# A Fourier mixer with two channel mixtures on one core: loads reordered behind the head, the second batch's first stage one spectral step sooner, decodes at other steps, all first-mixture statistics held

## The chip, the cores and the metric

The kernel runs on one core of a Trainium2 chip. The metric is device time in microseconds (us), the median of repeated executions. The profile shows one execution of the kernel before.

## What is computed

`x` has the shape (2, 3136, 256), in float32. Three blocks follow each other:

```python
X = rfft(x, axis=1)                                  # attention-like spectral filter
Y = soft(X.real@w_r - X.imag@w_i + b_r) + 1j*soft(X.real@w_i + X.imag@w_r + b_i)   # soft: shrink by 0.01
x = irfft(Y, n=3136, axis=1)
xn = (x - mean) / sqrt(var + 1e-6) * g_ln            # first mixture ("first MLP")
x = x + relu(xn @ w_ch1) @ w_ch2
u = x + real(fft(fft(x, axis=1), axis=2))            # second mixture
out = u + relu(norm(u) @ w2_ch1) @ w2_ch2
```

The mixture weights arrive as float64 words, and the kernel takes them apart into a high and a low float32 part itself ("decode").

## The kernel before, in words

The length 3136 is factored as 49 times 64. The work runs in this order on TensorE (PE), which is the engine that is nearly always busy.

1. **Head, stage 1 of batch 0.** `Forward` loads eight tiles of `x` (98 x 1024) and multiplies each half with the table `cam` (L331, plain float32, two passes each); VectorE (DVE) transposes the result out of PSUM (L333). Two steps of batch 1 (`fw[1]`, tiles named `q`) follow in the same plain form.
2. **Spectral steps.** The loop over `NS` = 26 steps calls `p2_step(i)`: `p2_b` multiplies two frequencies of the first stage with the table `cb` (L499, into one of three `psa` buffers) and splits the result into a high part (ScalarE, ACT) and a low part (DVE, L218); `p2_mix` of the step two before multiplies with the split filter weights `wm` (24 matmuls L532, into one of two `psb` buffers), and DVE adds the bias (L538) and clips (L539), GpSimd (POOL) subtracts (L218, `h<-w`); `p2_inv` of the step three before multiplies with `ci` (L553, into one of three `psc` buffers). A `psb` buffer is free again when its L538 is done.
3. **What rides along in that loop.** The dictionary `todo` hangs work on steps: `CONST_AT` the loads of tables (`cb`, `ci`, biases) and of `fw[1]` tiles, `MLP1_AT` the eight decodes of the first mixture's weights (`load_mlp`: a load `s64` of 512 KB, L569, then eight DVE instructions L581 to L589, function `decode64`). `behind` puts them after the latest clip and POOL subtraction that the program has marked. `STAGE1_AT[i]` says how many steps of stage 1 of batch 1 come in step i: each is split into `c` high (ACT) and `c` low (POOL) and multiplied in three matmuls (L228, L229, L230). The `q` tiles have three buffers, the `c` tiles four.
4. **First mixture.** 13 chunks of 3 or 4 tiles of 128 rows (`mlp1`), handled by `run_mlp`: `l1` is 8 groups of 6 matmuls (L228 to L230, into `psa`), each evacuated by ACT (L765) and then DVE (L767); `l2` is L784 and L785. While chunk k runs, the statistics (L664, L665), the normalisation (L672 to L676, applied by L691/L692 on ACT or L696 on DVE) and the flip (L705) of chunk k+2 are made. They hang on named places of chunk k; the table `EARLY` (chunks 11 and 12) places the statistics at the first two groups, `PLAIN` and `SHORT` (the others) later.
5. Stage 4 (98-row transforms, L228 to L230 into `psc`, L467 to L472) rides along from chunk 8, and the second mixture follows.

What puts instructions in order: a scheduler in the framework places each instruction on its engine by a modelled time, within the bounds of data, buffers and `tc.issue_after(...)`. Each engine then works strictly in that order, and so does SP, which issues all loads and stores. In `run_mlp`, `stats` is held behind the L767 of its own place by `issue_after(ch.rest[...])`, except where the plan has the key `"land"`, which only `EARLY` has.

Of the kernel before, what the change touches and what calls it, by code (L numbers as in the profile page):

```python
# [17 lines left out]


ZERO_AT = 12  # L20
STAGE1_AT = (0, 0, 0, 0, 2, 2, 2, 2, 2, 2, 2, 0)
STAGE3_FROM = 16
STAGE3_AT = (0,) * 16 + (4, 4, 4, 4)
CONST_AT = (0, 0, 1, 2, 2, 3, 4, 5, 6, 8)
MLP1_AT = (3, 8, 11, 12, 14, 15, 22, 23)
MLP2_AT = ((3, 7), (4, 2), (4, 7), (5, 2), (5, 7), (6, 4), (11, 1), (12, 3))
STAGE3_MLP = tuple((0, "l1", i) for i in (4, 5, 6, 7)) + tuple((0, "l2", i) for i in range(4)) + tuple(
    (1, "l1", i) for i in (1, 3, 5, 7)) + tuple((1, "l2", i) for i in range(4))
# [142 lines left out]
def fourier_moe_kernel(ctx, tc, x, w_r, w_i, b_r, b_i, g_ln, w11, w12, w21, w22,  # L171
# [14 lines left out]
    def hslot(dt=F32R):  # L186
        return wk.tile([128, 1024], dt, tag="h", name="h", bufs=HB)

    def qslot(dt=F32R):
        return wk.tile([128, 1024], dt, tag="q", name="q", bufs=3)  # L190
# [374 lines left out]
    def load64(src3, tag):  # L565

        s64 = wk.tile([128, 512], I64, tag=tag, name="s64", bufs=2)
        o = s64 if len(src3.shape) == 2 else s64.rearrange("p (f c) -> p f c", f=src3.shape[1])
        sp.dma_start(out=o, in_=src3)  # L569
        return s64  # L570
# [20 lines left out]
    def load_mlp(w1, w2, r, tag, two):  # L591

        srcs, raw = [], {}
        for i in range(4):
            c, h = divmod(i, 2)
            srcs.append((w1[c * 128:(c + 1) * 128, h * 512:(h + 1) * 512], i * 512))
        for i in range(4):
            srcs.append((w2[i * 256:(i + 1) * 256, :].rearrange("(f p) c -> p f c", p=128), 2048 + i * 512))  # L600

        def ask(k):
            if k < 8 and k not in raw:
                raw[k] = load64(srcs[k][0], tag)

        def piece(k):
            def f():
                ask(k)
                if two:
                    ask(k + 1)  # L610
                    t1, t2 = (wk.tile([128, 512], I32, tag="t98", name="t64", bufs=TB) for _ in range(2))
                elif k > 4:
                    ask(k + 1)
                    t1, t2 = (wk.tile([128, 512], I32, tag="r98", name="t64", bufs=R98) for _ in range(2))
                else:
                    ask(k + 1)
                    t = wk.tile([128, 2, 512], I32, tag="stg", name="t64", bufs=SB)
                    t1, t2 = t[:, 0, :], t[:, 1, :]
                o = srcs[k][1]
                if k < 4:  # L620
                    v = r.rearrange("p h f -> p (h f)")
                    decode64(raw[k], v[:, o:o + 512], v[:, 2048 + o:2560 + o], t1, t2)
                else:
                    v = w_views(r)[1][:, 2 * k - 8:2 * k - 6, :]
                    decode64(raw[k], v[:, :, 0:D], v[:, :, D:2 * D], t1, t2)
            return f

        return [lambda: ask(0)] + [piece(k) for k in range(8)]
# [290 lines left out]
    fw = [Forward(0, "a", lambda: hslot(F32)), Forward(1, "c", lambda: qslot(F32))]  # L919

    def l_cb(k, n):
        sp.dma_start(out=cb[:, k:k + n, :].rearrange("p k c -> p (k c)"), in_=t_cb[:, k * 128:(k + n) * 128])

    def l_ci(k, n):
        sp.dma_start(out=ci[:, k:k + n, :].rearrange("p k c -> p (k c)"), in_=t_ci[:, k * 128:(k + n) * 128])
# [36 lines left out]

    r3 = cp.tile([128, 2, 4096], F32R, tag="r3", name="r3a")
    wv1 = w_views(r3)
    mlp1_w = load_mlp(w11, w12, r3, "o", False)[1:]
    todo = {}

    def l_ca():
# [9 lines left out]
    def l_cd():  # L978
        tab["cd"] = cp.tile([128, 2, 129], F32, tag="cd", name="cd")
        sp.dma_start(out=flat(tab["cd"]), in_=t_cd)  # L980

    consts = [lambda: l_cb(7, 3), lambda: l_ci(4, 4),
              lambda: [fw[1].load(k) for k in range(1, 4)],
              lambda: l_cb(10, 7), lambda: l_ci(8, 8),
              lambda: l_cb(17, 8), lambda: l_ci(16, 8),
              lambda: (sp.dma_start(out=cb0, in_=t_cb0),
                       sp.dma_start(out=bias0[0:34], in_=b_r.unsqueeze(0).broadcast_to([34, D])),
# [4 lines left out]
              lambda: (l_cb(0, 1), l_ca())]  # L992
    for k, f in zip(CONST_AT, consts):
        todo.setdefault(k, []).append(f)
    for k, f in zip(MLP1_AT, mlp1_w):
        todo.setdefault(k, []).append(f)
    mlp1 = chunks1(0, wv1) + chunks1(1, wv1)
    mlp1[0].flipped = mlp1[1].flipped = False
# [20 lines left out]
    for i in range(NS + INV_BEHIND):  # L1019
        for f in todo.get(i, ()):  # L1020
            behind(f)
        for _ in range(STAGE1_AT[i] if i < len(STAGE1_AT) else 0):
            if fw[1].g % 2 == 0 and fw[1].g < 10:
# [9 lines left out]
        p2_step(i)  # L1033
        for e in range(STAGE1_AT[i + 1] if i + 1 < len(STAGE1_AT) else 0):
            with tc.issue_after(mark["hi"]), tc.issue_after(mark["pool"]):
# [25 lines left out]
    def run_mlp(chunks, nxt, hooks):  # L1061

        allc = chunks + nxt
        for k, ch in enumerate(chunks):
            n, m, far = (allc[k + d] if k + d < len(allc) else None for d in (1, 2, 3))
            at = {}

            def put(when, f, *a):
                part, i = when
                at.setdefault((part, min(i, ch.nt - 1) if part == "l2" else i), []).append(lambda: f(*a))  # L1070

            def split(c, ch=ch, n=n):
                with tc.issue_after(ch.relu), tc.issue_after(ch.rest[NF - 1]):
                    n.trans(c)

            def land(n, back):
                with ExitStack() as es:
                    if back is not None:
                        es.enter_context(tc.issue_after(back))
                    n.land()  # L1080

            if n is not None and n.flipped:
                if not n.landed:
                    put(LAND_AT, land, n, allc[k - 1].sent if k else None)
                for c in range(2):
                    put(("l2", 0), split, c)
            if m is not None:
                n_ = m
                if n_.front is not None:
                    pl = SOON if n_ is mlp2[0] else LATE if n_ is mlp2[6] else USUAL  # L1090
                    i = 0
                    for p, pr in enumerate(n_.front.pairs):
                        def stage_b(p, ch=ch, n_=n_):
                            with tc.issue_after(ch.pe):
                                n_.front.stage_b(p)

                        put(("l1", pl["b"][p]), stage_b, p)
                        put(("l1", pl["mix"][p]), n_.front.dmix, p, n_.y, i)
                        w = 2 if pr[0][1] else 1
                        for t in range(w):  # L1100
                            put(pl["stats"][p], n_.stats, i + t)
                        i += w
                else:
                    pl = EARLY if ch in mlp1[9:] else PLAIN if ch.nt == 4 else SHORT

                    def stats(t, ch=ch, n_=n_, when=pl["stats"], pl=pl):
                        with ExitStack() as es:
                            if "land" not in pl:
                                es.enter_context(tc.issue_after(ch.rest[when[t][1]]))
                            n_.stats(t)  # L1110

                    for t in range(4):
                        put(pl["stats"][t], stats, t)

                def norm(t, ch=ch, n_=n_, pl=pl):
                    with ExitStack() as es:
                        if n_.front is None and "land" not in pl:
                            es.enter_context(tc.issue_after(ch.relu))
                        if t == 0:
                            n_.norm()  # L1120
                        n_.apply(t)

                for t in range(4):
                    put(pl["norm"][t], norm, t)
                for h in range(2):
                    put(pl["flip"][h], n_.flip, h)
                if "land" in pl:
                    n_.landed = True
                    put(pl["land"], n_.land)
            soon = far is not None and far is not mlp1[6]  # L1130
            if soon:
                far.fetch()
            for f in range(NF):
                ch.l1(f)
                for h in at.get(("l1", f), []) + hooks.get((k, "l1", f), []):
                    h()
            for j in range(ch.nt):
                i = j if n is not None else ch.nt - 1 - j
                ch.l2(i)
                ch.store(i)  # L1140
                for h in at.get(("l2", j), []) + hooks.get((k, "l2", j), []):
                    h()
            if far is not None:
                if not soon:
                    far.fetch()
                if far.front is not None:
                    far.front.load()
# [123 lines left out]
```

## Time and profile before

| | |
|---|---|
| device time, median of 3 runs | 794.65 us (793.35 to 795.44) |
| the profiled execution | 795.71 us, of which the span of the trace is 793.7 us |
| PE busy | 780.3 us (98%), 4306 matmul records |
| DVE / ACT / POOL busy | 556.9 / 374.5 / 181.3 us |
| chain that ended last | PE 85%, DMA 6%, DVE 5% |

To read it: the engine with 98% bounds the kernel, so what can be gained without less arithmetic is PE's idle time and the time in which its clock is down. A busy PE is not PE at its peak, so idle time is found by the starts of neighbouring instructions and not by the busy sum alone. Times in the trace count from the start of the span.

### The profile page before, as it was taken

What the parts mean: (1) busy time and instruction counts of PE and PEld (TensorE: products, weight loads), DVE (VectorE), ACT (ScalarE), POOL (GpSimd) and SP (SyncE); (2) the same over time, 40 slices, a digit from 0 to 9 for tenths busy, and PEclk for the clock granted to TensorE, in tenths of its full rate; (3) what the DMA queues carried; (4) which work ended last, traced back from release to release, by engine and by line L of the source; (5) the groups of instructions that cost most, each with busy time, mean ns of one, the idle gap of its engine ahead of it and who ended that gap; (6) DMA issues with size and microseconds to landing.
All of it is one profiled execution on the core that took longest, in us unless ns stands there. A gap on an engine that the chain in (4) does not pass through costs nothing.

```text
span 793.7 us, 12135 instructions
## 1 busy us (share of the span) xinstructions
PE 780.3 (98%) x4306; PEld 664.4 (84%) x4306; DVE 556.9 (70%) x1253; ACT 374.5 (47%) x807; POOL 181.3 (23%) x198
## 2 busy tenths in 40 slices
PE   9899999999999999999999999999999999999997
PEld 3789987988888888988788898888888898888886
DVE  6499987678865889868765887555655757666643
ACT  0354356447954444457333336554643535444421
POOL 0176321254511111144430001566400000000000
PEclk9999999999999999999999999999999999999999
DMA  8822210630247233355643336554543334322211
GB/s 239 258 75 84 65 49 1 209 117 28 80 146 275 70 127 120 115 149 187 207 149 98 106 109 159 151 164 139 150 133 93 112 123 121 101 77 76 61 33 40
DMA packets 78911, 95.16 MB, mean 120 GB/s; under 512 B 17538, under 2 KB 59274, under 8 KB 78656
## 3 DMA queue, kind: packets, MB, share of 16 engines
q1 hardware_dynamic: 78772, 94.33, 39.2%
q8 instruction: 34, 0.56, 0.3%
q14 instruction: 25, 0.20, 0.1%
q10 hardware_dynamic: 80, 0.07, 0.0%
HBM read 56.89 MB, written 37.49 MB: 119 GB/s over the span
## 4 chain that ended last, share of the span: by engine, by line
PE 85%; DMA 6%; DVE 5%; SPq 1%; issue 1%; POOL 1%; ACT 1%; DVEq 0%; POOLq 0%
PE psb L784 23%; PE psb L785 12%; PE psa L228 11%; PE psa L229 11%; PE psa L230 11%; PE psb L532 4%; PE psc L852 3%; DMA q<-in_x_dram 2%; PE psc L230 2%; PE psc L368 2%; PE psc L228 2%; DMA s<-in_moe_w_ch_dram 2%; PE psc L229 2%; PE psc L877 1%; PE psa L499 1%; PE psc L553 1%
## 5 line engine op out<-in xcount | busy, mean ns | idle before, releaser
L765 ACT ACTIVATE h<-psa 128x512 fp32r<-128x512 f32 (+2 forms) x208 | 117.3, 572 | 199.9 <-PE psa L230 146.6
L767 DVE SCALAR_TENSOR_TENSOR h<-psa,h 128x512 fp32r<-128x512 f32 (+2 forms) x208 | 135.1, 654 | 61.1 <-ACT h L765 58.1
L784 PE MATMUL psb<-r3a,h 128*128 128x512 f32 x392 | 137.1, 395 | 0.0
L784 PE MATMUL psb<-r2b,h 128*128 128x512 f32 x392 | 136.8, 397 | 0.0
L785 PE MATMUL psb<-r3a,h 128*128 128x256 f32 x392 | 106.2, 281 | 0.0
L785 PE MATMUL psb<-r2b,h 128*128 128x256 f32 x392 | 105.9, 281 | 0.0
L532 PE MATMUL psb<-wm,h 128*128 128x256 f32 (+1 forms) x600 | 92.1, 298 | 0.6 <-DVE w L538 0.6
L532 PEld LDWEIGHTS psb<-wm,h 128*128 128x128 f32 (+1 forms) x600 | 79.0, 188 | 8.5 <-issue 6.4
L784 PEld LDWEIGHTS psb<-r2b,h 128*128 128x128 f32 x392 | 71.7, 188 | 15.7 <-issue 0.6
L784 PEld LDWEIGHTS psb<-r3a,h 128*128 128x128 f32 x392 | 71.9, 188 | 15.1
L228 PE MATMUL psa<-u0r,r3a 128*128 128x512 f32 (+1 forms) x208 | 80.0, 385 | 1.9 <-DVE h L767 1.9
L228 PE MATMUL psa<-u0r,r2b 128*128 128x512 f32 (+2 forms) x208 | 80.6, 387 | 0.0
L229 PE MATMUL psa<-u0r,r3a 128*128 128x512 f32 (+1 forms) x208 | 79.0, 381 | 0.0
L229 PE MATMUL psa<-u0r,r2b 128*128 128x512 f32 (+2 forms) x208 | 78.5, 378 | 0.0
L230 PE MATMUL psa<-u0r,r2b 128*128 128x512 f32 (+2 forms) x208 | 78.0, 380 | 0.0
L785 PEld LDWEIGHTS psb<-r3a,h 128*128 128x128 f32 x392 | 73.9, 189 | 4.0
L785 PEld LDWEIGHTS psb<-r2b,h 128*128 128x128 f32 x392 | 74.0, 189 | 3.3
L230 PE MATMUL psa<-u0r,r3a 128*128 128x512 f32 (+1 forms) x208 | 76.6, 380 | 0.0
L790 DVE TENSOR_TENSOR o<-psb,yb 128x256 f32<-128x256 f32 x74 | 30.2, 418 | 57.5 <-PE psb L785 56.2
L210 ACT ACTIVATE yg<-psc 98x512 f32<-98x512 f32 (+2 forms) x58 | 49.5, 872 | 30.4 <-PE psc L553 14.7
L218 POOL TENSOR_TENSOR u0r<-w,u0r 98x512 fp32r<-98x512 f32 (+2 forms) x28 | 37.4, 1349 | 95.5 <-ACT u0r L210 94.5
L218 POOL TENSOR_TENSOR h<-w 128x512 f32<-128x512 f32 (+1 forms) x26 | 34.7, 1334 | 93.0 <-DVE w L539 64.4
(141 smaller groups left out, 1369.8 us busy)
## 6 DMA issues: line engine op xcount, KB each, us to landing
dT<-q SPq DMA_DIRECT2D x19, 512.0 KB
q<-dT SPq DMA_DIRECT2D x19, 512.0 KB
s<-in_moe_w_ch_dram SPq DMA_DIRECT2D x16, 512.0 KB
dA<-o SPq DMA_DIRECT2D x32, 196.0 KB
dY<-yg SPq DMA_DIRECT2D x12, 512.0 KB
r<-dA SPq DMA_DIRECT2D x48, 128.0 KB
dX<-o SPq DMA_DIRECT2D x10, 512.0 KB
yb<-dX SPq DMA_DIRECT2D x50, 64.0 KB
```

The source lines that it names most:

```text
L210: nc.scalar.activation(out=o, in_=i, func=AF.Copy, scale=scale)
L218: ins = eng.tensor_tensor(out=o, in0=a, in1=b, op=ALU.subtract)
L228: nc.tensor.matmul(out=ps, lhsT=lh, rhs=rh, start=first, stop=False)
L229: nc.tensor.matmul(out=ps, lhsT=ll, rhs=rh, start=False, stop=False)
L230: ins = nc.tensor.matmul(out=ps, lhsT=lh, rhs=rl, start=False, stop=last)
L532: nc.tensor.matmul(out=ps[0:m, u * D:(u + 1) * D], lhsT=xv[:, o:o + m], rhs=wm_hl[wv][:, e, c, :], start=k == 0, stop=k == 11)
L765: ins = nc.scalar.activation(out=h[:, 0:n], in_=ps[:, 0:n], func=AF.Relu)
L767: ins = nc.vector.scalar_tensor_tensor(out=l[:, 0:n], in0=ps[:, 0:n], scalar=0.0, in1=h[:, 0:n], op0=ALU.max, op1=ALU.subtract)
L784: nc.tensor.matmul(out=ps, lhsT=h[:, ts_], rhs=w2[:, f, :], start=f == 0, stop=False)
L785: ins = nc.tensor.matmul(out=ps[:, 0:D], lhsT=l[:, ts_], rhs=w2[:, f, 0:D], start=False, stop=f == NF - 1)
L790: nc.vector.tensor_tensor(out=o, in0=ps[:, 0:D], in1=self.y[:, i, :], op=ALU.add)
L852: nc.tensor.matmul(out=ps, lhsT=self.raw[p][0:n, k, q * 128:(q + 1) * 128], rhs=self.cols(n, pr[k][1], im), start=True, stop=True)
```

## The change

It is made in four tables and three places of the code. The number of instructions on every engine stays as it was; their order moves.

- `STAGE1_AT`: the seven double steps of batch 1's stage 1 come in spectral steps 3 to 9 instead of 4 to 10.
- `CONST_AT` and `consts`: the first raw weight load (`mlp1_w[0]`) is asked for right behind `cb` 7 to 9; `fw[1].load(1)` comes before `ci` 4 to 7; loads 2 and 3 come one by one behind `cb` 10 to 16.
- `MLP1_AT`: the decodes hang on steps 3, 7, 10, 11, 12, 14 instead of 3, 8, 11, 12, 14, 15 (the last two as before).
- `stats` in `run_mlp`: the statistics of chunks 11 and 12 are now held as the others are.

```diff
-STAGE1_AT = (0, 0, 0, 0, 2, 2, 2, 2, 2, 2, 2, 0)
+STAGE1_AT = (0, 0, 0, 2, 2, 2, 2, 2, 2, 2, 0)
-CONST_AT = (0, 0, 1, 2, 2, 3, 4, 5, 6, 8)
-MLP1_AT = (3, 8, 11, 12, 14, 15, 22, 23)
+CONST_AT = (0, 0, 0, 0, 1, 1, 2, 3, 4, 5, 6, 7, 8)
+MLP1_AT = (3, 7, 10, 11, 12, 14, 22, 23)
-    mlp1_w = load_mlp(w11, w12, r3, "o", False)[1:]
+    mlp1_w = load_mlp(w11, w12, r3, "o", False)
-    consts = [lambda: l_cb(7, 3), lambda: l_ci(4, 4),
-              lambda: [fw[1].load(k) for k in range(1, 4)],
-              lambda: l_cb(10, 7), lambda: l_ci(8, 8),
+    consts = [lambda: l_cb(7, 3), mlp1_w[0], lambda: fw[1].load(1), lambda: l_ci(4, 4),
+              lambda: l_cb(10, 7), lambda: fw[1].load(2), lambda: fw[1].load(3), lambda: l_ci(8, 8),
-    for k, f in zip(MLP1_AT, mlp1_w):
+    for k, f in zip(MLP1_AT, mlp1_w[1:]):
-                            if "land" not in pl:
-                                es.enter_context(tc.issue_after(ch.rest[when[t][1]]))
+                            es.enter_context(tc.issue_after(ch.rest[when[t][1]]))
```

**Place 1, the loads on SP behind the head.** Before, from the load of `cb` 7 to 9 on (`s64` is a raw weight load, `q` a tile of batch 1):

```order
L922 DMA cb_77<-in_cb_dram 128x384
L925 DMA cw_82<-in_ci_dram 128x512
L309 DMA q_208<-in_x_dram 98x1024
L309 DMA q_210<-in_x_dram 98x1024
L309 DMA q_212<-in_x_dram 98x1024
L922 DMA cb_77<-in_cb_dram 128x896
L925 DMA cw_82<-in_ci_dram 128x1024
L922 DMA cb_77<-in_cb_dram 128x1024
L569 DMA s64_270<-in_moe_w_ch1_dram 128x512
```

And in the changed kernel, from the same load on:

```order
L922 DMA cb_77<-in_cb_dram 128x384
L569 DMA s64_196<-in_moe_w_ch1_dram 128x512
L309 DMA q_198<-in_x_dram 98x1024
L925 DMA cw_82<-in_ci_dram 128x512
L922 DMA cb_77<-in_cb_dram 128x896
L309 DMA q_213<-in_x_dram 98x1024
L309 DMA q_226<-in_x_dram 98x1024
L925 DMA cw_82<-in_ci_dram 128x1024
L569 DMA s64_279<-in_moe_w_ch1_dram 128x512
L309 DMA q_290<-in_x_dram 98x1024
```

The first raw weight load moved from eighth place behind `cb` 7 to 9 to first, and two of the three `q` loads went behind the next `cb` load.

**Place 2, the first decode on DVE.** Before, from the last split of the first three spectral steps on (the decode is L581 to L589 on `t64`):

```order
L218 TENSOR_TENSOR h_228<-psa_229,h_227 128x4x128
L538 TENSOR_TENSOR w_264<-psb_238,cw_82 128x512
L539 TENSOR_SCALAR w_265<-w_264 128x512
L581 TENSOR_SCALAR t64_274<-s64_270 128x512
L584 TENSOR_SCALAR t64_274<-s64_270 128x512
L583 SCALAR_TENSOR_TENSOR t64_274<-s64_270,t64_274 128x512
L538 TENSOR_TENSOR w_320<-psb_294,cw_82 128x512
L218 TENSOR_TENSOR h_284<-psa_285,h_283 128x4x128
```

And in the changed kernel:

```order
L218 TENSOR_TENSOR h_229<-psa_230,h_228 128x4x128
L581 TENSOR_SCALAR t64_281<-s64_196 128x512
L584 TENSOR_SCALAR t64_281<-s64_196 128x512
L583 SCALAR_TENSOR_TENSOR t64_281<-s64_196,t64_281 128x512
L585 SCALAR_TENSOR_TENSOR r3a_191<-t64_281 128x512
L586 TENSOR_SCALAR t64_281<-s64_196 128x512
L588 TENSOR_SCALAR t64_281<-r3a_191 128x512
L538 TENSOR_TENSOR w_265<-psb_239,cw_82 128x512
L587 SCALAR_TENSOR_TENSOR t64_281<-s64_196,t64_281 128x512
L539 TENSOR_SCALAR w_266<-w_265 128x512
```

Six of the eight decode instructions now stand ahead of the first bias addition L538; before, the decode stood between the first clip and the second L538. On PE the first split step of batch 1 (L228 on `c98_270`) now stands behind the 33rd of the first 40 L532 that follow the fourth `p2_b`; before, it stood behind all 40 and 27 further L532, eight L499 and two L553.

**Place 3, the statistics on DVE at the start of chunk 9 of the first mixture.** One piece of the difference; the first L767 above it is that of chunk 9's first group:

```order
-L790 TENSOR_TENSOR o<-psb,yb 128x256
-L705 STREAM_TRANSPOSE q<-q 128x4x4x32 x2
-L791 TENSOR_TENSOR o<-psb,o 128x256
-L471 TENSOR_TENSOR o_1758<-o_1758,psc 98x2x127
-L767 SCALAR_TENSOR_TENSOR h<-psa,h 128x512
-L472 TENSOR_TENSOR o_1758<-o_1758,psc 98x2x127
-L664 BN_STATS st<-yb 128x6 x3
+L664 BN_STATS st<-yb 128x6 x2
+L665 BN_AGGR mv<-st 128x2 x2
+L790 TENSOR_TENSOR o<-psb,yb 128x256
+L791 TENSOR_TENSOR o<-psb,o 128x256
```

The statistics of the three tiles of chunk 12 (`x3`) leave chunk 9 for chunk 10, and those of the four tiles of chunk 11 (`x2`, and a second `x2` behind the next L767) come from chunk 8 into chunk 9.

## Rows read from the trace of the kernel before

**Rows 1.** The page, busy time of the engines.

```profile
PE 780.3 (98%) x4306; PEld 664.4 (84%) x4306; DVE 556.9 (70%) x1253; ACT 374.5 (47%) x807; POOL 181.3 (23%) x198
```

**Rows 2.** Timeline of PE, head: start us, us, what, form, xcount [idle before <-releaser].

```profile
25.57 5.04 PE L532 MATMUL psb<-wm,h 128*128 128x256 f32 x40
30.45 0.61 PE L499 MATMUL psa<-cb,yg 128*128 128x128 f32 x4
32.70 1.16 PE L499 MATMUL psa<-cb,yg 128*128 128x128 f32 x8 [1.64 <-DMA cb<-in_cb_dram]
...
37.44 0.61 PE L499 MATMUL psa<-cb,yg 128*128 128x128 f32 x4
38.60 0.59 PE L532 MATMUL psb<-wm,h 128*128 128x256 f32 x3 [0.56 <-DVE w L538]
40.08 0.50 PE L228 MATMUL psc<-c,cam_hl 98*128 98x512 f32 x1 [0.89 <-ACT c L210]
...
46.05 0.84 PE L532 MATMUL psb<-wm,h 128*128 128x256 f32 x5
47.80 0.50 PE L228 MATMUL psc<-c,cam_hl 98*128 98x512 f32 x1 [0.91 <-ACT yg L210]
48.14 0.40 PE L229 MATMUL psc<-c,cam_hl 98*128 98x512 f32 x1
48.93 0.50 PE L230 MATMUL psc<-c,cam_hl 98*128 98x512 f32 x1 [0.40 <-POOL c L218]
```

**Rows 3.** Timeline of DVE in the same stretch.

```profile
25.29 0.69 DVE L218 TENSOR_TENSOR h<-psa,h 128x512 fp32r<-128x512 f32 x1 [0.48 <-ACT h L210]
...
28.73 0.69 DVE L538 TENSOR_TENSOR w<-psb,cw 128x512 f32<-128x512 f32 x1 [2.75 <-PE psb L532]
...
36.49 0.43 DVE L581 TENSOR_SCALAR t<-s 128x512 int32<-128x512 int32 x1 [6.61 <-DMA s<-in_moe_w_ch_dram]
...
37.77 0.68 DVE L538 TENSOR_TENSOR w<-psb,cw 128x512 f32<-128x512 f32 x1
```

**Rows 4.** The chain that ended last, in order of time: start us, us, what.

```profile
19.12 4.87 DMA cb<-in_cb_dram
24.01 12.46 DMA s<-in_moe_w_ch_dram
```

**Rows 5.** Timeline across the start of chunk 9's third group (PE, DVE).

```profile
381.37 1.08 DVE L664 BATCH_NORM_STATS2 st<-yb 128x6 f32<-128x256 f32 x3 [3.57 <-DMA yb<-dY]
...
383.92 0.39 PE L230 MATMUL psa<-u0r,r3a 128*128 128x512 f32 x1
...
385.47 0.68 DVE L767 SCALAR_TENSOR_TENSOR h<-psa,h 128x512 fp32r<-128x512 f32 x1
...
386.20 0.79 PE L228 MATMUL psa<-u0r,r3a 128*128 128x512 f32 x1 [1.89 <-DVE h L767]
...
389.72 0.39 PE L230 MATMUL psc<-u0r,ca_hl 98*98 98x512 f32 x1
```

**Rows 6.** Stretches: window, PE, PEld, DVE, ACT, POOL busy (x), PEclk, DMA, GB/s.

```profile
380.00:382.00 2.00, 2.00 (x10) 1.65 (x9) 0.63 (x2) 0.01 (x1) 0.00 (x0) 1.00 0.37 122
...
386.20:389.70 3.50, 3.50 (x8) 2.66 (x9) 3.43 (x9) 0.54 (x1) 0.56 (x1) 0.51 0.98 313
```

**Rows 7.** Timeline of DVE in chunk 10, from the end of an `l2` tile.

```profile
409.21 0.42 DVE L790 TENSOR_TENSOR o<-psb,yb 128x256 f32<-128x256 f32 x1 [1.14 <-PE psb L785]
...
411.71 0.69 DVE L767 SCALAR_TENSOR_TENSOR h<-psa,h 128x512 fp32r<-128x512 f32 x1 [0.17 <-ACT h L765]
...
413.07 0.69 DVE L767 SCALAR_TENSOR_TENSOR h<-psa,h 128x512 fp32r<-128x512 f32 x1 [0.34 <-ACT h L765]
```

**Rows 8.** One group of DVE by line, 54 to 110 us: xcount, busy us, mean ns, idle before.

```profile
L588 DVE TENSOR_SCALAR t<-r3a 128x512 int32<-128x512 int32 x5 | 4.3, 857 | 0.0
```

**Rows 9.** Timeline of DVE, one decode instruction alone and one stretched.

```profile
80.08 0.42 DVE L588 TENSOR_SCALAR t<-r3a 128x512 int32<-128x512 int32 x1
...
88.11 1.51 DVE L588 TENSOR_SCALAR t<-r3a 128x512 int32<-128x512 int32 x1
```

## The prediction

> **What bounds the kernel now.** I read the page first: PE is busy for 780.3 us of a span of 793.7 us, every other engine far less [rows 1]. The change neither adds nor takes away an instruction on any engine, so only PE's lost time can be won, and it has to be found first. A busy sum hides it, so I went through the starts of neighbouring PE instructions. Two places carry nearly all that can move: the head between 30 and 50 us, and one spot at 384 to 390 us.
>
> In the head PE waits five times, for a transfer, DVE, ACT and POOL [rows 2]. A pass of L532 takes 0.122 us (40 from 25.57 to 30.45), one of L499 0.11, one of 512 columns 0.23. From the end of the passes before to the next start, the waits are 30.89 to 32.70 (a `cb` load), 37.88 to 38.60 (DVE's L538), 38.97 to 40.08 (ACT), 46.66 to 47.80 (ACT), 48.37 to 48.93 (POOL): 1.81 + 0.72 + 1.11 + 1.14 + 0.56 = 5.34 us.
>
> Why those engines are late is told by DVE [rows 3]: it stands still for 6.61 us until a raw weight load (`s64`) lands at 36.5, because the first decode stands in its queue. The bias addition L538 behind it starts at 37.77, and the splits that ACT and POOL make for PE come late with it. The chain says the same: that load takes 12.46 us from its issue [rows 4].
>
> At the second place DVE again waits for a transfer, 3.57 us, with the statistics of chunk 12 at the head of its queue [rows 5]. The L767 behind them starts at 385.47, and PE, which needs that `psa` buffer, starts at 386.20 instead of 384.15: 2.05 us. Then the granted clock is 0.51 in the next 3.5 us, the lower of the two levels (1.2 GHz), after PE had stood still, while just before it was 1.00 [rows 6]. Eight passes from 386.20 to 389.72 take 3.52 us where the full clock needs about half, 1.80: 1.72 us more. Together 3.77 us.
>
> **The change part by part.** *Loads on SP.* Rates first. Between the landing of `cb` 7 to 9 (19.12 + 4.87 = 23.99) and that of the raw load (36.47) lie, by the order, 256 + 3 x 392 + 448 + 512 + 512 + 512 = 3416 KB in 12.48 us: 274 KB/us [rows 4]. In the new order 512 KB follow `cb` 7 to 9 at once: an estimate of 23.99 + 1.9 = 25.9 us for the first raw load. Bounds: 25.2 at half as much again per us, and 32.0 if it took 12.46 us from its issue at 19.5 as before. I take 25.9, as the queue in front of it is the same up to the load before. The `q` tile behind it: 904 KB, 27.3 us. `cb` 10 to 16: before, 1880 KB after 23.99 until PE went on at 32.70, that is 216 KB/us; now 1608 KB, so 31.4 (29.9 at 274 KB/us).
>
> The rule that speaks against this is in the Trainium skill, "DMA: Bandwidth & Descriptors", section "Queues, rings and completion order": one transfer is split over several engines' rings, and completion isn't first in, first out per issuing engine, so a place in SP's queue is no landing time. By it the load could land as late as its slowest ring; the trace agrees in part, since the late landing of `cb` 10 to 16 is slower than the mean rate. It is the first rival.
>
> *First decode.* DVE's last split ends at 25.98 [rows 3], so the load is there. Three of the six decode instructions took 1.28 us (36.49 to 37.77); the other three take another 1.3 if none is stretched, 2.4 if one is as L588 at times (0.42 alone, 1.51 stretched [rows 9]). That is 28.6 to 29.7, and the L538 behind them could not start before 28.73 anyway, when PE delivers [rows 3]. The decode fits into a 2.75 us gap in which DVE was idle; cost about 0, at most 1.0 us of DVE time. The second L538 then comes near 31.3, when PE has finished its 40 passes and the two of L228/L229 between them, instead of 37.77.
>
> *Stage 1 of batch 1 a step sooner.* PE comes to its first split matmul at 25.57 + 33 x 0.122 = 29.6; the `q` tile is there at 27.3 and needs one ACT copy, room 1.6 us. PE comes to the second frequency of the fifth step (the first to read `cb` 10) at 31.3, the load lands at 29.9 to 31.4: of the 1.81 us wait 0 to 0.1 remain. Behind it PE takes the next `psb` buffer at 32.2; the L538 that frees it is done by 30.4. So all five waits lose their cause. What is late next is POOL: it makes one `h` and two `c` per step, the same per step as before. The `c` low parts wait for it, and SP's later `q` loads wait for these in turn, since `q` has three buffers: the fourth (`q_290`) can be issued only once both halves of `q_198` are split. Queued behind `q_290` is `cb` 17 to 24; its first reader, step 8, is some 20 us away at PE's pace of 5 to 6 us per step, so nothing there reaches PE. I take off 0.1 us for `cb` and nothing else: **5.2 us** won, bounds 0 and 5.34.
>
> *Decodes 1 to 4 at steps 7, 10, 11, 12.* Same instructions. DVE is full in this stretch (its groups show no idle time ahead of the decode instructions [rows 8]), and three decodes now follow each other without a step between. But DVE gains the 6.61 us in which it stood and the 2.75 us gap, some 9 us, while PE comes only 5.2 us sooner. Cost 0; if this cover is gone, the rival of crowding.
>
> *Hold of the statistics.* The wait of 3.57 us and with it the 3.77 us of PE go, as chunk 12's statistics now come a chunk later, with the landing at 381.4 far behind them. Added is DVE work where none was: in chunk 9 four statistics and the norm of chunk 11, in chunk 10 three statistics, norm and three applies of chunk 12, between the L767 of the second and third group. PE needs the third group's `psa` buffer only at the sixth group, three groups of 6 x 0.23 = 1.4 us and a stage-4 triple later. In chunk 10 the third L767 starts at 411.71, 2.5 us after the tile's addition at 409.21 [rows 7]; it now has about ten short instructions ahead of it, of 0.1 to 0.4 us each, and comes 1 to 1.5 us later. Two groups' time covers that. In chunk 9 ACT's eight apply instructions stand ahead of its evacuations too, and I see hardly any room left there: I take off 0.4 us, bounds 0 and the 3.77 of today. **3.4 us** won.
>
> The sum against the profiled execution's own time: 795.71 - 5.2 - 3.4 = 787.1 us. That execution is 1.06 us above the median of the runs; the same 8.6 us off the median of 794.65 gives **786.0 us**.
>
> **The rivals.**
>
> *Late first load.* Six decode instructions now stand ahead of the first L538 instead of behind it. If the load lands at t, L538 ends at t + 2.6 + 0.6, and PE, which wants that buffer at 32.2, loses t - 29.0. At the upper bound of 32.0 that is 3.0 us: 789.0. For it: the 12.46 us of before and the late `cb`. Against: up to its end 512 KB are queued behind `cb` 7 to 9, where it was 3416 KB. The same mechanism ends on the other side: all 8.6 us are gone at t = 37.6, and from t = 40 the kernel is slower by more than 0.3%, to 799 at t = 42. It decides on one landing.
>
> *A new wait in chunks 9 and 10.* If DVE or ACT is late by 2 us there, PE stops again and the clock falls again as at 386.20; the 3.77 us are paid as today, and 795.71 - 5.2 - 1.06 = 789.4 remains. For it: the thin room in chunk 9. Against: nothing waits for a transfer any more.
>
> *Crowding of the decodes.* L588 has a mean of 857 ns [rows 8] where it takes 420 alone, so decode instructions are stretched by something, and stage 1's POOL work comes beside them. With two stretched instructions of 1.1 us per piece, three pieces in a row cost DVE 6.6 us; less the 4 us that DVE wins on PE, and about 1.5 us until a late clip holds up L553 through POOL, 1 to 4 us of the gain go: 787 to 790. Here the Trainium skill, "SBUF — State Buffer", section "Who interferes with whom", says that a DVE instruction in its two-port mode and a GpSimd instruction exclude each other for their whole length. The stretches of 1.1 us agree with it, though no row here names POOL as their cause; by that rule alone every decode instruction that meets one of POOL's could be hit, the dearer end of this rival.
>
> *It does nothing.* If PE's waits in the head had another common cause (say the rate at which POOL makes splits), the earlier order would only move them: then 5.2 us stay lost, 790.9, from the hold alone.
>
> **How the numbers follow.** A measurement of this kernel can tell about 0.3% (2.4 us) from no change, so faster means under 792.3. Forecast 0.70 (faster). Late load 0.10: 0.06 faster, 0.02 same, 0.02 slower. New wait in chunks 9 and 10 0.09: 0.08 faster, 0.01 same. Crowding 0.07: 0.05 faster, 0.01 same, 0.01 slower. Does nothing 0.04: 0.02 faster, 0.01 same, 0.01 slower. Sum: 0.91 faster, 0.05 same, 0.04 slower. The range begins at 784.5 (both gains whole, 9.1 us, and 1 us of spread between runs) and reaches to 790.5, which takes in the first three rivals' near ends.
>
> **What would show it.** Right: in the changed profile DVE's first L581 starts near 26 with little or no wait for `s`, the first L538 near 28.7, the second near 31; PE shows no idle over 0.5 us between 30 and 50; at chunk 9 no DVE wait for `yb`, and the granted clock stays at 1.00 from 376 to 392. Wrong: a DVE wait for `s` of over 3 us ahead of the first L538; PE idle on POOL `c` or `h` between 40 and 100; a PE wait on L767 in chunks 9 or 10 with a stretch of half clock behind it; a stall at a place that has none today.

## The result and the profile after

| | kernel before | changed kernel |
|---|---|---|
| device time, median | 795.05 us (793.35 to 796.25, 4 runs) | 787.89 us (787.28 to 789.16, 4 runs) |
| the profiled execution | 795.71 us, span 793.7 us | 788.44 us, span 786.6 us |

The ratio is 0.9914, 95% interval 0.989 to 0.9937: 0.9% faster, or 7.2 us where 8.6 were forecast; the time lies near the forecast of 786.0 us and inside its range. Two later measurements of the same kernel on other chips gave 0.9908 and 0.9914.

The busy times of the engines, to be set beside [rows 1]:

```profile
PE 778.3 (99%) x4306; PEld 662.7 (84%) x4306; DVE 557.8 (71%) x1253; ACT 374.4 (48%) x807; POOL 180.9 (23%) x198
```

PE's sum fell by 2.0 us only, while the span fell by 7.1: a busy sum does not tell lost time. So here, and in all runs below, "lost" means: from the start of one PE instruction to the start of the next, less the median of that gap for the same line and shape. It holds waits and slow clock alike; a gap across the border of two stretches goes to one of them, which moves up to 0.2 us. Before, 16.97 us are lost in the whole span; after, 9.99.

The head, timeline of PE (columns as in [rows 2]). The gaps of [rows 2] are gone: between 22.5 and 58 us no row carries a wait.

```profile
20.72 1.98 PE L331 MATMUL psc<-q,cam 98*128 98x512 f32 x4 [0.49 <-DMA q<-in_x_dram]
22.54 2.84 PE L499 MATMUL psa<-cb,yg 128*128 128x128 f32 x24
...
32.32 1.50 PE L499 MATMUL psa<-cb,yg 128*128 128x128 f32 x12
...
58.70 0.47 PE L228 MATMUL psc<-c,cam_hl 98*128 98x512 f32 x1 [0.58 <-DVE yg L333]
```

Two small waits are new. The first tile of batch 1 begins at 20.72 with a wait for its load, and decode 1 makes PE wait at 58.70.

The same stretch on DVE (to [rows 3]). The first decode instruction L581 has no wait for `s`, and the L538 behind six of them comes 2.8 us after the end of the last split.

```profile
26.70 0.69 DVE L218 TENSOR_TENSOR h<-psa,h 128x512 fp32r<-128x512 f32 x1 [0.48 <-ACT h L210]
27.31 0.42 DVE L581 TENSOR_SCALAR t<-s 128x512 int32<-128x512 int32 x1
...
30.15 0.69 DVE L538 TENSOR_TENSOR w<-psb,cw 128x512 f32<-128x512 f32 x1
...
32.52 0.69 DVE L538 TENSOR_TENSOR w<-psb,cw 128x512 f32<-128x512 f32 x1
```

Chunk 9 of the first mixture, DVE (to [rows 5]). At its second group the statistics are those of chunk 11, without a wait; PE's third group is served by the L767 at 379.17.

```profile
373.56 0.69 DVE L767 SCALAR_TENSOR_TENSOR h<-psa,h 128x512 fp32r<-128x512 f32 x1
374.16 0.74 DVE L664 BATCH_NORM_STATS2 st<-yb 128x6 f32<-128x256 f32 x2
...
379.17 0.68 DVE L767 SCALAR_TENSOR_TENSOR h<-psa,h 128x512 fp32r<-128x512 f32 x1
```

The stretch around it (columns as in [rows 6]): PE busy throughout, the clock 1.00 where it was 0.51.

```profile
376.00:392.00 16.00, 16.00 (x78) 12.89 (x77) 12.52 (x27) 10.73 (x30) 7.98 (x8) 1.00 0.71 233
```

Where the time came from, as lost time by stretch (us):

| stretch | before | after |
|---|---|---|
| 0 to 30, loads of `x` | 0.40 | 1.70 |
| 30 to 60, head | 5.81 | 0.88 |
| 60 to 145 | 1.04 | 0.41 |
| 145 to 180 | 1.98 | 2.26 |
| 375 to 400, chunk 9 | 3.85 | 0.25 |
| the rest | 3.89 | 4.49 |

### The profile page after: what moved, and what is told of

It is laid out like the page before. It is cut to its first block, busy times and chain, and to the rows that moved or that the text cites. A ratio compares the mean times of both kernels' runs of the same rounds, so it can differ in the third digit from the quotient of the medians.

```text
span 786.6 us, 12135 instructions
## 1 busy us (share of the span) xinstructions
PE 778.3 (99%) x4306; PEld 662.7 (84%) x4306; DVE 557.8 (71%) x1253; ACT 374.4 (48%) x807; POOL 180.9 (23%) x198
## 4 chain that ended last, share of the span: by engine, by line
PE 89%; DVE 4%; DMA 3%; issue 1%; SPq 1%; ACT 0%; POOL 0%; POOLq 0%; DVEq 0%
PE psb L784 23%; PE psb L785 12%; PE psa L228 12%; PE psa L230 11%; PE psa L229 11%; PE psb L532 5%; PE psc L852 3%; PE psc L228 2%; PE psc L230 2%; PE psc L229 2%; PE psc L368 2%; PE psa L499 2%; PE psc L877 1%; DMA q<-in_x_dram 1%; PE psc L553 1%
## 5 line engine op out<-in xcount | busy, mean ns | idle before, releaser
L767 DVE SCALAR_TENSOR_TENSOR h<-psa,h 128x512 fp32r<-128x512 f32 (+2 forms) x208 | 135.1, 654 | 61.9 <-ACT h L765 58.5
L532 PE MATMUL psb<-wm,h 128*128 128x256 f32 (+1 forms) x600 | 90.4, 297 | 0.1
L532 PEld LDWEIGHTS psb<-wm,h 128*128 128x128 f32 (+1 forms) x600 | 78.1, 188 | 7.6 <-issue 5.5
L228 PE MATMUL psa<-u0r,r2b 128*128 128x512 f32 (+2 forms) x208 | 80.6, 388 | 0.0
L228 PE MATMUL psa<-u0r,r3a 128*128 128x512 f32 (+1 forms) x208 | 79.5, 382 | 0.0
```

What stands on the lines that cost most here:

```text
L228: nc.tensor.matmul(out=ps, lhsT=lh, rhs=rh, start=first, stop=False)
L532: nc.tensor.matmul(out=ps[0:m, u * D:(u + 1) * D], lhsT=xv[:, o:o + m], rhs=wm_hl[wv][:, e, c, :], start=k == 0, stop=k == 11)
L767: ins = nc.vector.scalar_tensor_tensor(out=l[:, 0:n], in0=ps[:, 0:n], scalar=0.0, in1=h[:, 0:n], op0=ALU.max, op1=ALU.subtract)
```

## The experiments

Three sets of runs, each on one chip with its own runs of the kernel before: the first gave 797.81 us for it, the second 797.82, the third 796.57.

**First set: the parts apart.** Theory: the order of the loads makes the head's gain, the hold that of chunk 9, and the two add up. Rival: a common cause, so that one part alone gives little.

`e1_hold_only`, the kernel before with the hold alone:

```diff
-                            if "land" not in pl:
-                                es.enter_context(tc.issue_after(ch.rest[when[t][1]]))
+                            es.enter_context(tc.issue_after(ch.rest[when[t][1]]))
```

> The kernel before with only the hold of the statistics of chunks 11 and 12. Theory (two separate gains): the DVE wait for yb of 3.6 us in chunk 9 and PE's 3.6 to 3.8 us with it are gone, the head keeps its DVE wait of 6.6 us for the raw load: 795.05 - 3.7 = 791.4 us, 790.9 to 792.0. Rival (the wait only moves to chunk 9's or 10's L767 by the work that is added there): 794 to 795 us, with a PE wait on L767 and a stretch of half clock in the profile.

`e2_tables_only`, the changed kernel with those lines as before:

> The changed kernel without the hold. Theory (two separate gains): the head is as in the changed kernel, chunk 9 as in the kernel before, so the sum of this gain and that of the hold alone is the whole 7.2 us: 787.9 + 3.7 = 791.6 us, 790.9 to 792.2. Rival (the two depend on each other, since everything behind the head comes some 4 us earlier while the transfer of yb need not): the wait in chunk 9 is longer than 3.6 us by what the head won, 793 to 795 us.

`e3_loads_only`, the same, with two tables put back also, so that only the order of the loads differs from the kernel before:

```diff
-STAGE1_AT = (0, 0, 0, 2, 2, 2, 2, 2, 2, 2, 0)
+STAGE1_AT = (0, 0, 0, 0, 2, 2, 2, 2, 2, 2, 2, 0)
-MLP1_AT = (3, 7, 10, 11, 12, 14, 22, 23)
+MLP1_AT = (3, 8, 11, 12, 14, 15, 22, 23)
```

> Only the order of the loads is new; stage 1 of batch 1, the decode steps and the statistics as in the kernel before. Theory (the raw load's place alone made the waits of the head): DVE's wait for s is gone, the five PE waits too, 790.8 to 792.2 us, as without the hold. Rival (the earlier stage 1 fills PE where it would wait): PE still waits 2 us or more between 30 and 50 us, 793 to 794.5 us.

`a0_again`, the changed kernel:

> The changed kernel once more, on the same chip as the three above. Theory for the 1.3 us by which its first head ran later than that of the kernel before (20.7 against 19.4 us at batch 1's first tile): spread between executions, since the first 19 loads are the same; then the start of that tile differs between the runs of this call without regard to the kernel. Rival (the new order disturbs the head): here and in every kernel with the new load order it starts at 20.5 us or later, in the others at 19.5. Time 787 to 789 us either way.

| | median, us | ratio, 95% interval | lost 30 to 60 | lost 60 to 145 | lost 375 to 400 |
|---|---|---|---|---|---|
| hold only | 795.30 | 0.9976, 0.9959 to 0.9993 | 5.82 | 0.91 | 0.24 |
| tables only | 791.34 | 0.9921, 0.9905 to 0.9937 | 0.92 | 0.48 | 1.25 |
| loads only | 792.22 | 0.9938, 0.9917 to 0.996 | -0.03 | 1.92 | 1.29 |
| changed | 789.95 | 0.9908, 0.9894 to 0.9922 | 1.03 | 0.49 | 0.21 |

The loads alone empty the head and give 5.6 of the 7.9 us between the medians (the profiled execution of loads only was its slowest, 795.90 us, so its other stretches are on the high side). The hold does what was said of its place, yet it is worth less than the 3.7 us expected: 2.5 us by the medians of hold only, 1.4 us from tables only to changed. Why stands in the two traces without it. DVE, chunk 9, of tables only; loads only has the same wait of 0.83 us, at 376.93:

```profile
373.12 1.08 DVE L664 BATCH_NORM_STATS2 st<-yb 128x6 f32<-128x256 f32 x3 [0.83 <-DMA yb<-dY]
```

Where this wait is 0.83 us, [rows 5] have 3.57. From SP's issue (369.5 and 373.4) the load landed after some 3.6 us; in the first profile it was issued at 375.1 and took 6.3. That left open whether the new order of loads or chance shortened it.

**Second set: the landing of `yb`, the two tables, and the price of a late first load.**

`b0_before` is the kernel before, unchanged; it has a median of its own beside that of the runs it is compared with.

> The kernel before, unchanged, for a second profile. The hold alone won 2.5 us by the medians where 3.4 were forecast, and the two runs without the hold showed DVE waiting only 0.83 us for yb (landing 3.5 us after its issue) where the first profile of before had 3.57 us (6.3 us). Theory (the first profile caught a slow landing of yb): DVE waits 0.8 to 1 us here, PE loses 0.5 to 1.3 us between 380 and 390 us instead of 3.75, and the granted clock stays at 1.00 there. Rival (the new order of the loads shortened it in the other runs): DVE waits over 3 us again, PE loses over 3 us with a stretch of half clock. Either way the five head waits between 30 and 50 us are there, 5 to 6 us together.

`e4_stage1_back`:

```diff
-STAGE1_AT = (0, 0, 0, 2, 2, 2, 2, 2, 2, 2, 0)
+STAGE1_AT = (0, 0, 0, 0, 2, 2, 2, 2, 2, 2, 2, 0)
```

> The changed kernel with batch 1's first stage at its old steps. Theory (the head gain comes from the place of the raw load and of the cb loads alone): no PE idle over 0.5 us between 30 and 50 us, time within 0.5 us of the changed kernel. Rival (the earlier stage gives work that fills a gap): PE idle of 1 us or more between 40 and 60 us, or at the tail of the first stage, 1 to 2 us slower than the changed kernel.

`e5_decodes_back`:

```diff
-MLP1_AT = (3, 7, 10, 11, 12, 14, 22, 23)
+MLP1_AT = (3, 8, 11, 12, 14, 15, 22, 23)
```

> The changed kernel with the decodes 1 to 5 at their old steps 8, 11, 12, 14 and 15. Theory (decode 1 at step 7 holds DVE and makes PE wait 0.58 us for yg at 58.7): that wait goes, and nothing comes for it: 0 to 0.7 us faster than the changed kernel. Rival one (crowding, the three decodes in a row cost DVE): 1 to 3 us faster. Rival two (the later decodes make the tail of the first mixture late): PE waits for POOL's h (L553) from 80 to 165 us grow by 0.5 to 1.5 us, and the kernel is as much slower.

`e6_late_raw`:

```diff
-CONST_AT = (0, 0, 0, 0, 1, 1, 2, 3, 4, 5, 6, 7, 8)
+CONST_AT = (0, 0, 0, 1, 1, 2, 3, 2, 2, 5, 6, 7, 8)
-    consts = [lambda: l_cb(7, 3), mlp1_w[0], lambda: fw[1].load(1), lambda: l_ci(4, 4),
+    consts = [lambda: l_cb(7, 3), lambda: fw[1].load(1), lambda: l_ci(4, 4),
-              lambda: l_cb(17, 8), lambda: l_ci(16, 8),
+              lambda: l_cb(17, 8), mlp1_w[0], lambda: l_ci(16, 8),
```

> The changed kernel with the first raw weight load put behind cb 17 to 24 (and the seventh behind cb 7 to 9), so that 2904 KB stand between cb 7 to 9 and it. Theory (the landing of this one load decides the head): it lands near 34.6 us, DVE stands still for 7 to 8 us from 26.7, PE loses landing minus 29.0, about 5.6 us, between 32 and 50 us, and the time is 5 to 6 us above the changed kernel's. Rival (a place in the queue is no landing time, the load comes when its rings are free): it lands before 30 us and the time is within 1 us. Rival two (DVE's late L538 is not what holds PE): the landing is late, but PE's idle between 32 and 50 us is under 2 us.

| | median, us | ratio, 95% interval | lost 30 to 60 | lost 60 to 145 | lost 375 to 400 |
|---|---|---|---|---|---|
| before again | 796.55 | 0.9979, 0.9958 to 0.9999 | 6.37 | 0.43 | 1.46 |
| stage 1 back | 791.64 | 0.9927, 0.9902 to 0.9952 | -0.07 | 4.32 | 0.25 |
| decodes back | 787.74 | 0.9877, 0.9853 to 0.99 | -0.04 | 0.23 | 0.23 |
| late raw load | 797.61 | 0.9998, 0.9984 to 1.0013 | 8.78 | 1.18 | 0.23 |

*Before again.* The same code measured against itself reads 0.2% off, so a difference of that size, such as that of the hold alone (0.9976), is not shown by medians. Its trace answers the question on `yb`; DVE:

```profile
380.53 1.08 DVE L664 BATCH_NORM_STATS2 st<-yb 128x6 f32<-128x256 f32 x3 [0.79 <-DMA yb<-dY]
```

Issued at 377.0, the load landed after 3.5 us. The new order is not the cause: the first profile had drawn a slow landing. By the updates of its semaphore, fifteen of that load's sixteen parts had landed by 378.95 and the last came at 381.34; here the last two came at 380.37 and 380.50. PE loses 1.46 us in this stretch, not 3.85. The five waits of the head are all there.

*Late raw load.* DVE and PE:

```profile
36.88 0.43 DVE L581 TENSOR_SCALAR t<-s 128x512 int32<-128x512 int32 x1 [10.15 <-DMA s<-in_moe_w_ch_dram]
```

```profile
39.63 4.85 PE L532 MATMUL psb<-wm,h 128*128 128x256 f32 x21 [6.32 <-DVE w L538]
```

One landing decides the head. At 36.9 us instead of before 27.3 all that the change brings is gone (ratio 0.9998). No row of the head carries a wait for `cb`, so the five waits of before are here one long wait for DVE. The prediction's price, landing minus 29.0, gives 7.9 us; PE waited 6.32, as it came to the place 1.1 us later than forecast and L538 was done sooner, and another 2.5 us went in passes at half clock behind the wait. So the 8.78 us lost come near the price partly by chance.

The landing came 2.3 us later than my estimate from 2904 KB at 274 KB/us. Most of that is not the rate: the semaphore of `cb` 7 to 9 tells its landing at 25.68 here and at 24.00 in before. Counted from there the raw load took 11.2 us for 2904 KB, and in before 12.5 us for 3416 KB ([rows 4]); at 274 KB/us it would be 10.6. The rule of the Trainium skill quoted in the prediction ("DMA: Bandwidth & Descriptors", section "Queues, rings and completion order"), that completion is not first in, first out per issuing engine, is not borne out here: the load landed 1.26 us behind `cb` 17 to 24, which was issued just before it and landed at 35.60.

*Stage 1 back* fell for the rival by its trace (its median has no changed kernel beside it in this set), and shows the crowding that the prediction priced. POOL, then DVE, then PE of that trace:

```profile
78.56 1.38 POOL L218 TENSOR_TENSOR h<-w 128x512 f32<-128x512 f32 x1 [2.50 <-DVE w L539]
```

```profile
78.73 1.48 DVE L588 TENSOR_SCALAR t<-r3a 128x512 int32<-128x512 int32 x1
...
80.74 1.08 DVE L333 STREAM_TRANSPOSE yg<-psc 128x512 f32<-128x512 f32 x1
```

```profile
79.99 1.13 PE L553 MATMUL psc<-h,cw 128*128 128x256 f32 x4 [1.09 <-POOL h L218]
```

The transposes L333 of stage 1 still stand among three decodes in a row, DVE has no idle row, the clip L539 comes at 78.06, and PE waits for what POOL makes of it. The L588 at 78.73 begins within a POOL instruction and ends 0.3 us behind its end (79.94). It is no single case: of the 32 instructions of L581, L584, L586 and L588 between 20 and 150 us of this trace, eight took over 0.7 us; all eight began within a POOL instruction and ended 0.28 to 0.29 us behind its end, and none of the other 24 began within one. In before seven are stretched so, in the changed kernel six, in decodes back four. The Trainium skill, "SBUF — State Buffer", section "Who interferes with whom", has two-port DVE instructions and GpSimd exclude each other for a whole instruction; this trace agrees, and now with POOL's own rows beside DVE's.

Of the two tables, then, lost time from 50 to 60 and from 60 to 100 us:

| | decodes at old steps | decodes at new steps |
|---|---|---|
| stage 1 at old steps | 0.02 and 1.86 (loads only) | -0.10 and 4.38 (stage 1 back) |
| stage 1 a step sooner | 0.07 and 0.36 (decodes back) | 1.00 and 0.56 (changed) |

The earlier stage 1 is the useful one of the two: it takes the transposes out of the way of the decodes. The new decode steps cost more than they bring, here 1.1 us. The lower row repeats: from 50 to 100 us four traces with the decodes at old steps (decodes back, and three of the third set below) lose 0.33 to 0.44 us, four with them at new steps (three of changed, tables only) 1.52 to 1.57. The upper row has one trace for each cell.

**Third set: is there a better version, and the hold once more.** `a1_after` is the changed kernel, `e5b_decodes_back` repeats the edit of `e5_decodes_back`.

> The changed kernel once more, beside three others on the same chip: ratio to the kernel before 0.991 as in its two earlier measurements (0.9914 and 0.9908), PE waiting 0.58 us for yg near 58 us.

> The changed kernel with decodes 1 to 5 at their old steps, as once before (then 0.9877 of the kernel before, on another chip than the changed kernel's 0.9908). Theory (only the wait for yg at 58 us goes with it): 0.5 to 1 us faster than the changed kernel in this call. Rival (the three decodes in a row cost more in places that one profile does not show): 2 us or more faster. Second rival (the chips differ): no difference.

`e7_prep_later`, the decodes back and besides:

```diff
-PREP0_AT = (23, 24, 26, 28)
+PREP0_AT = (24, 24, 26, 28)
```

> The decodes back, and also the statistics of the very first chunk of the mixture a spectral step later (24 instead of 23), so that a split, a bias addition and a clip stand ahead of them on DVE, where DVE now stands 5.2 us from 146.9 to 152.1 us for the load of stg. Theory (that standstill makes PE's waits of 2.3 us between 150 and 170 us, as the first raw load made those of the head): these waits shrink to under 0.8 us, and the kernel is 1 to 2 us faster than with the decodes back alone. Rival (the first chunk's normalisation then comes late): a new PE wait of 1 to 3 us between 162 and 175 us, on the flipped tile or on u0r, and no gain.

`e8_e5_no_hold`, the decodes back, and the two lines of the hold as before:

> The decodes back, and the hold taken away again: the price of the hold a third time, and a third draw of the landing of yb. Theory (the hold is worth the usual short landing: DVE waits 0.8 us for yb, PE loses 0.5 us there and as much again at slower passes): 1 to 1.5 us slower than with the decodes back and the hold; clock 1.00 between 380 and 400 us. Rival (the first profile of before was the usual case): DVE waits over 3 us, 3 to 4 us slower.

| | median, us | ratio, 95% interval | lost 145 to 180 | lost 375 to 400 | lost 500 to 530 |
|---|---|---|---|---|---|
| changed | 789.51 | 0.9914, 0.9901 to 0.9926 | 2.30 | 0.27 | 1.01 |
| decodes back | 789.96 | 0.9918, 0.9906 to 0.9931 | 2.52 | 0.27 | 4.40 |
| also first statistics later | 788.03 | 0.9893, 0.988 to 0.9906 | 0.71 | 0.27 | 2.04 |
| decodes back, no hold | 790.02 | 0.9923, 0.991 to 0.9936 | 2.52 | 1.59 | 0.24 |

*Decodes back* is not faster this time: in its trace the 58.70 wait is gone, but a stall at 515 us, far from the edit, takes more. It is again a load at the head of a queue, POOL's, that lands after it is wanted; POOL and PE:

```profile
515.26 0.72 POOL L416 TENSOR_TENSOR w<-stg 98x254 f32<-98x254 f32 x1 [7.40 <-DMA stg<-dX]
```

```profile
518.20 0.48 PE L230 MATMUL psc<-u0r,ca_hl 98*98 98x512 f32 x1 [2.40 <-POOL u0r L218]
```

This load was not slow: it took 6.7 us from its issue at 508.59, and 6.5 in the trace without the hold, where it was issued at 506.73. SP came to it late. So the 1.1 us that the decodes' steps cost is read from the traces; whether the medians follow stays open (787.74 in one set, no difference in the other).

*First statistics later* beats both kernels. The place is a third copy of the one fault: DVE standing until 152 us for `stg`, in the changed kernel of this set and then with the edit:

```profile
152.69 1.41 DVE L664 BATCH_NORM_STATS2 st<-stg 128x6 f32<-128x256 f32 x4 [5.07 <-DMA stg<-dY]
```

```profile
151.91 1.41 DVE L664 BATCH_NORM_STATS2 st<-stg 128x6 f32<-128x256 f32 x4 [0.37 <-DMA stg<-dY]
```

With a split, a bias addition and a clip ahead of the statistics, PE's lost time there falls from 2.52 (decodes back) and 2.30 (changed) to 0.71, and the runs lie at 787.35 to 788.46 us, all below those of decodes back (from 788.62) and of the changed kernel (from 788.78).

*No hold*: PE loses 1.59 us at chunk 9 instead of 0.27, with a wait of 1.14 us for `yb`. The medians differ by 0.1 us all the same. The two traces differ most at 515 us, where the one with the hold lost 4.40 us, but it is the slowest execution of its five and does not explain a median. From 500 to 530 us four of the five traces without the hold lost 0.2 to 0.5 us (loads only 1.82), and eight of the nine with it over 0.5, up to 4.40. So the hold may give back there what it wins at chunk 9; no run tests this.

## Why the prediction was right, and where it was off

- *The head, 5.2 us forecast.* Right. Lost time from 30 to 60 us went from 5.81 to 0.88, 4.9 us. The cause, the raw load at the head of DVE's queue, is shown from both sides: the loads alone take the loss away, and the raw load put back behind `cb` 17 to 24 (the loads around it move with it) brings it back.
- *"The load is there" at DVE's last split.* Right, by a small margin: the load landed at 27.03, 1.8 us behind `cb` 7 to 9 where 1.9 were forecast, and DVE took it up at 27.31. In three other traces of the new order (tables only, changed, stage 1 back) DVE waited 0.32 to 0.49 us for it, without a wait of PE. The first L538 came at 30.15, not near 28.73, since the whole head stood 1.4 us later; from the end of the last split it took 2.76 us, as before.
- *Waits for `cb`, second L538, POOL.* Right: no wait for `cb`, no wait for POOL's `c`, no idle of PE up to 58 us. The 0.1 us for `cb` was not needed.
- *"Cost 0" for the decodes at steps 7, 10, 11, 12.* Wrong in size. The argument was that DVE gained 9 us of standstill; but that lies at 26 to 36 us, and decode 1 meets DVE's transposes at 56 us. Cost: a PE wait of 0.58 us at 58.70, a stall at a place that had none and so one of the prediction's own signs of being wrong, and 1.1 us of lost time from 50 to 100.
- *Stage 1 a step sooner* was priced only by its risks. Its gain, 2.7 us beside the new decode steps (4.38 - 0.10 against 1.00 + 0.56 in the table of four above), was not seen. Crowding is shown, but in the version without this part.
- *The hold, 3.4 us forecast.* Right against the first profile (3.85 to 0.25), wrong as a typical price. The size came from one landing of `yb`: DVE's wait was 3.57 us there, and 0.79, 0.83, 0.83 and 1.14 in four other traces without the hold. The usual price is 1.0 to 1.3 us of PE's time (1.25 to 1.59 lost in those four traces, less 0.25). The 0.4 us taken off for chunk 9's thin room was not lost there: 0.25 us remain. That the pair of profiles gave 3.6 us, so near the 3.4, is luck: the base happened to hold the slow landing, and by the usual price the forecast is 2.2 us too high here.
- *The sum, 787.1 us against 788.44 for the profiled execution.* The miss of 1.3 us is as large as what the loads of `x` took more in this execution (0.40 to 1.70 up to 30 us). In the other traces that stretch cost 0.20 to 3.25 us whatever the order; the profile before had a low draw.
- *The rivals.* Late load: its point of balance (37.6 us forecast; at 36.9 the ratio is 0.9998) comes out, its price in parts by chance as said above; its condition did not arise. New wait in chunks 9 and 10: none. Does nothing: refuted; its 790.9 us is also a slip, as the 3.4 us of the hold off 794.65 give 791.3.

That the medians still moved by 7.2 us with a hold of 1.2 in place of 3.4 is not settled piece by piece; the medians of one unchanged kernel differ by 1.3 us within a set. In the traces, lost time in the whole span is 16.97 and 16.76 us in the two of the kernel before and 9.99, 11.06 and 10.50 in the three of the changed one, 6.3 between the means. The clock has its share: the two traces of before and that of hold only each have, behind the first 6 us, one stretch of 3.4 us at half clock, 1.7 us lost, at chunk 9 in the first and in the head in the other two (from 50.2 and from 42.4 us). So the 1.72 us that the prediction gave to chunk 9 belong to no fixed place. The three of the changed kernel have none before their last microsecond. The mean granted clock of the runs agrees: 0.9978 for the kernel before (17 runs of the first set) and 0.9992 for the changed one (5 runs), 0.14% or 1.1 us.

## What to carry to other kernels

An instruction that waits for a transfer at the head of an in-order queue costs whatever is queued behind it; move the load forward or the instruction back, and look for further copies of the same pattern (here at 30, 380, 152 and 515 us). A wait for a transfer in one profile is a single draw: before a price is put on it, compare the time from issue to landing in a second profile; a late issue and a slow transfer look the same from the engine that waits. A table that moves filler work is priced at the place where the work lands, not by the idle time that was won elsewhere.

## What was not expected of the hardware

After a standstill PE's granted clock sometimes falls to the lower level and sometimes not, and the length of the wait alone does not order the cases. Stretches of the windows view (window, PE, PEld, DVE, ACT, POOL busy, PEclk, DMA share, GB/s): first of before, around and after the waits of 1.81, 0.72 and 1.11 us of [rows 2].

```profile
32.00:36.00 4.00, 3.30 (x26) 3.27 (x27) 0.00 (x0) 0.00 (x0) 0.00 (x0) 1.00 0.99 395
36.00:40.00 4.00, 2.63 (x18) 2.19 (x17) 3.51 (x8) 0.91 (x3) 0.00 (x0) 1.00 0.14 55
```

Then of hold only, whose head is that of before. Its timeline has idle times of 1.56, 0.58 and 0.88 us for the same three waits, where that of before has 1.64, 0.56 and 0.89.

```profile
42.40:45.80 3.40, 3.40 (x13) 2.92 (x11) 3.40 (x4) 1.11 (x4) 3.36 (x3) 0.50 0.00 0
```

Last of the loads-only run, behind a wait of 1.51 us (up to 10.33) among the first loads; and of the late raw load, behind 6.32 us.

```profile
10.20:14.50 4.30, 4.17 (x6) 1.84 (x7) 2.00 (x2) 0.00 (x0) 0.00 (x0) 0.60 0.92 237
```

```profile
40.00:44.00 4.00, 4.00 (x20) 4.00 (x20) 4.00 (x7) 0.42 (x1) 3.28 (x3) 0.50 0.00 0
```

Nearly the same three waits were followed by full clock in one execution and by half in the other. A wait of 1.81 us was followed by full clock, one of 1.51 us by half. What the drop added: in the late raw load 8.78 us were lost around a wait of 6.32.

The rows also show two rates of loading: 395 GB/s in 32 to 36 us of before, where tables and weights of 128 partitions are moved, and 237 GB/s in the loads-only row above, where it is mostly the tiles of `x` with 98 partitions. By the trace's records of single packets, one of 4096 bytes took 163 ns on average in the first stretch and 253 ns in the second. Why is not shown.
